# Attention and expert layers in one kernel: all four att-v chunks of a pair in one block, tail scores in a bank of their own

## The chip, the cores and the metric

The kernel runs on one core of a Trainium2 chip. The time is the device time of one execution in microseconds. The engines are named as in the profile: TensorE (PE; PEld is its weight load), VectorE (DVE), ScalarE (ACT), GpSimd (POOL) and SyncE (SP), whose queue issues most transfers. Matrix products write to PSUM, which has eight banks per partition; VectorE and ScalarE read them out.

## The reference, cut to what matters

```python
# q, k, v: 8 batches x 12 heads x 448 positions x 64, fp32
scores = q @ k.T / sqrt(64) - log(448)
attn = 1 / (1 + exp(-scores))                  # a sigmoid, no row sums
x = concat_heads(attn @ v)                     # 3584 tokens x 768
# 8 experts, w1 768 x 1024, w2 1024 x 768
logits = normalise(x) @ normalise(expert_emb).T / tau
e = argmax(logits); gate = softmax(logits)[e]
out = gate * (relu(x @ w1[e]) @ w2[e])         # each token through one expert
```

## The kernel before, in words

**Pairs of heads.** The attention loop runs over 48 pairs: 8 batches times 6 pairs of heads. The 448 positions of a pair are three chunks of 128 and a tail of 64 per head. For a pair i the loop does

- `turn(i + 2, 1)` and `turn(i + 2, 0)` (L336, L327): four fp32 transposes each, for k and for q of the pair after next. VectorE or ScalarE splits the result into a high and a low fp16 part (L344, L346, L347).
- `scores(i, c)` (L358) for c = 0, 1, 2: six products per chunk, three terms for two heads side by side in row halves of the array. ScalarE's sigmoid (L360) reads them out.
- `scores_tail(i)` (L367): three products for the tails of both heads, and their sigmoid (L369).
- `av(i, c)` (L380): fp32 products of the sigmoids with v, two heads side by side in column halves, four chunks (0, 1, 2 and the tail CM = 3) into one accumulator bank.
- `evac(i)` (L394 on ScalarE, L396 on VectorE): the accumulator into xT, high and low part.

Before, chunks 2 and CM of pair i - 1 are multiplied in the loop's pass for pair i, behind its scores 0 and 1; chunks 0 and 1 of pair i come at the end of the pass.

**Work between the pairs.** When the six pairs of a batch are done, `batch_tasks` lists work that the following passes take up, one list each: `chunk` (L402) computes the router's logits of 128 tokens with 12 small products, which VectorE reduces (L404); seven chunks cover two batches. Then `route1` and `route2` (rank products L446, L447), once `select` (L467) and once `early1` (L499) with products that count tokens per expert. `rows` writes token rows to memory with a transposing transfer; `norm` (L421 on VectorE, L424 on ScalarE) squares them. From the fifth batch on, VectorE also casts expert weights: a high part (L170) and a low part (L174), a chunk of 128 rows of w1 or w2 per pass.

**PSUM.** Scores and tail scores take turns in two double banks (`pss`), att-v in two banks (`psv`), and transposes, logits and rank products take turns in two banks that share the tag `tr` (`ptr`, `psl`, `psr`): each new tile takes the bank used longest ago, when its readers are through.

**Order.** In the loop TensorE and SP run in the order in which the program is written. VectorE's, ScalarE's and POOL's queues are ordered by the scheduler. Behind the loop come the first layer-1 halves of two early expert tiles (`layer1_full`, L213; their copies L244 and L246), the last batch's logits and routing, and then 33 expert tiles.

Of the kernel before, what the change touches and what calls it, by code (L numbers as in the profile page):

```python
# [12 lines left out]
F32 = mybir.dt.float32  # L13
I32 = mybir.dt.int32
AF = mybir.ActivationFunctionType
ALU = mybir.AluOpType
AX = mybir.AxisListType
ET = mybir.EngineType
PSUM = bass.MemoryType.PSUM
DRAM = bass.MemoryType.DRAM  # L20

P = 128
CM = 3
# [4 lines left out]
NP = H // 2  # L28
NT = B * S
DM = H * D  # L30
E = 8
# [14 lines left out]
GE = 2  # L46
GC = P * JG
N0 = 4
EG = 5
ORD = "aGbLcdCDAMB"  # L50
ED = 2

# [57 lines left out]
def attn_moe_kernel(ctx: ExitStack, tc: tile.TileContext, q, k, v, emb, tau, w1, w2, consts, eye, out, dbg=None):  # L110
# [3 lines left out]
    dpool = ctx.enter_context(tc.tile_pool(name="dpool", bufs=1, space=DRAM))  # L114
    stg = ctx.enter_context(tc.tile_pool(name="stg", bufs=4))
    ps_s = ctx.enter_context(tc.tile_pool(name="ps_s", bufs=2, space=PSUM))
    ps_v = ctx.enter_context(tc.tile_pool(name="ps_v", bufs=2, space=PSUM))
    mctx = ExitStack()
    ps_m = mctx.enter_context(tc.tile_pool(name="ps_m", bufs=2, space=PSUM))
    wpool = ctx.enter_context(tc.tile_pool(name="wpool", bufs=1))  # L120
# [140 lines left out]
    with ExitStack() as actx:  # L261
# [100 lines left out]

        def scores_tail(i):
            x = kq[i]
            ps = ps_s.tile([P, 2, 512], F32, name="pss")[:, 0, :S]
            for n, (ki, qi) in enumerate(QK_TERMS):
                nc.tensor.matmul(ps, x[:, ki, SM:512], x[:, qi, 512:], start=(n == 0), stop=(n == 2))  # L367
            a = ap2.tile([P, S], F32, name="att_t", bufs=2)
            sig[0] = nc.scalar.activation(a, ps, AF.Sigmoid, bias=bias_s, scale=1.0 / (8.0 * SQK * SQK))  # L369
            aa[i, CM] = a  # L370
# [3 lines left out]
        def av(i, c):  # L374
            if c == 0:
                pav[i] = ps_v.tile([P, 512], F32, name="psv")
            a = aa.pop((i, c))
            for h in range(2):
                w, m = (vv[i][:, h, c, :], a[:, h, :]) if c < CM else (tails[i // TB % 2][2][:, i % TB, h, :], a)
                nc.tensor.matmul(pav[i][h * D:(h + 1) * D, :S], w, m, start=(c == 0), stop=(c == CM))  # L380

        xTs = {}

        def evac(i):
            b, hp = pairs[i]
            ps = pav.pop(i)[:, :S]
            if b % 2 == 0 and hp == 0:
                xTs[b // 2] = ap2.tile([P, JG, 2, NP, P], F16, name="xT")
            x = xTs[b // 2]
            j0 = b % 2 * (CM + 1)  # L390
            parts = ((ps[:, main(b)].rearrange("d (j r) -> d j r", j=CM), [x[:, j0:j0 + CM, ii, hp, :] for ii in range(2)]),
                     (ps[:, tail(b)], [x[:, CM, ii, hp, b % 2 * HP:(b % 2 + 1) * HP] for ii in range(2)]))
            for src, (hi, lo) in parts:
                mark[ET.Activation] = nc.scalar.activation(hi, src, AF.Copy, scale=SX)  # L394
            for src, (hi, lo) in parts:
                mark[ET.DVE] = nc.vector.scalar_tensor_tensor(lo, src, SX, hi, op0=ALU.mult, op1=ALU.subtract)  # L396

        def chunk(g, j):
            ps = ps_m.tile([P, 2 * E], F32, tag="tr", name="psl")
            for kc in range(NKC):  # L400
                for ii in range(2):
                    nc.tensor.matmul(ps, xTs[g][:, j, ii, kc, :], enT[:, kc, :],  # L402
                                     start=(kc == 0 and ii == 0), stop=(kc == NKC - 1 and ii == 1))
            nc.vector.tensor_reduce(L[:, g * JG + j], ps.rearrange("p (i e) -> p e i", i=2), axis=AX.X, op=ALU.add)  # L404
            rowq.append((g, j))

        def rows(g, j):
            xr = xrp.tile([P, 2, DM], F16, name="xrow", bufs=4)
# [123 lines left out]
        def batch_tasks(b):  # L532
            g = b // 2
            if b % 2 == 0:
                return [[lambda j=j: chunk(g, j)] for j in range(3)]
            r = [[lambda: chunk(g, 3), lambda: chunk(g, 4)], [lambda: chunk(g, 5), lambda: chunk(g, 6)],
                 [lambda: route1(g)], [lambda: route2(g)]]
            if g == GS:
                r += [[select]]
            if g == GE:  # L540
                r += [[early1]]
                todo.append((EG, early2))
            return r
# [37 lines left out]
        def task():  # L581
            if later or fill:
                (fill or later).pop(0)()

        with tc.manual_schedule(engines={ET.SP, ET.PE}):
            for i in range(NPAIR):
# [8 lines left out]
                    rows(*rowq.pop(0))  # L595
                scores(i, 0)
                scores(i, 1)
                if i > 0:
                    av(i - 1, 2)
                    av(i - 1, CM)  # L600
                    evac(i - 1)
                if soon:
                    for f in soon.pop(0):
                        f()
                if i + 2 < NPAIR:
                    turn(i + 2, 1)
                task()
                scores_tail(i)
                if i + 2 < NPAIR:
                    turn(i + 2, 0)  # L610
                task()
                scores(i, 2)
                av(i, 0)
                av(i, 1)
                if i + 3 < NPAIR:
                    pack(i + 3, 1)
                    pack(i + 3, 0)
                task()
                if i > 0:
                    b, hp = pairs[i - 1]  # L620
                    if hp == NP - 1:
                        soon = batch_tasks(b)
                if i + 3 == NPAIR:
                    qctx.close()
                    bw = ctx2.enter_context(tc.tile_pool(name="bw", bufs=1, side="right", reuse_waits="tile"))
# [23 lines left out]
        ph[0] = ps_s.tile([P, 2, 512], F32, name="pss")  # L649
        layer1_full(-2, 0, xte[0], 0)  # L650
        hidden(-2, 0)
        for c in (2, CM):
            av(NPAIR - 1, c)
        evac(NPAIR - 1)
        po = {0: [None, None]}
        po[0][0] = ps_v.tile([P, 512], F32, name="psv")
        ph[1] = ps_s.tile([P, 2, 512], F32, name="pss")
# [147 lines left out]

    layer1_full(-1, 0, xte[1], 1)
    hidden(-1, 1)
    po[0][1] = ps_v.tile([P, 512], F32, name="psv")
    hs = [hT.pop((-2, half)) for half in range(2)]
    layer2_full(0, hs, po[0], (0, 3 * NFC // 2))  # L810
    with tc.high_priority():
# [210 lines left out]
```

## Time and profile before

| | us |
|---|---|
| median of 3 runs | 880.82 |
| lowest and highest run | 879.9, 886.85 |
| profiled execution, its own time | 877.93 |
| its span | 876.1 |
| TensorE busy | 826.9 (94%) |
| VectorE busy | 395.7 (45%) |
| ScalarE busy | 398.3 (45%) |

Times in the profile are microseconds from the span's start, unless marked ns. A row of the order of time gives start, length, engine, line and operation, the tiles written and read, shapes, and in brackets the engine's idle time before it with what ended it; neighbouring like instructions are merged (x12). Lengths of TensorE's instructions overlap, since its products are pipelined; the distance between two starts is what a block takes. The attention loop goes from about 10 to 348 us of the span.

### The profile page before, as it was taken

To read this page: it belongs to the slowest core of one execution; us is meant where nothing else is said; L and a number is where in the kernel's file an instruction comes from. 1 tells how busy PE (TensorE), PEld (TensorE's weight loads), DVE (VectorE), ACT (ScalarE), POOL (GpSimd) and SP (SyncE) were. 2 spreads that over 40 slices of the span, in tenths; PEclk is the share of its full clock that TensorE was granted. 3 is DMA by queue.
4 is the path that set the end of the run, shared out by engine and by line. 5 is a ranking of instruction groups with operands and counts; after the bars stand their busy time and mean duration, and the time that the engine had idled before them with its cause. 6 is when DMAs were issued, how large, how long until landed. Compare 5 with 4: busy or idle time off the path is not lost. (4 is left out here: it accounts for less than half of the span.)

```text
span 876.1 us, 16426 instructions
## 1 busy us (share of the span) xinstructions
PE 826.9 (94%) x5384; PEld 402.8 (46%) x5384; DVE 395.7 (45%) x759; ACT 398.3 (45%) x610; POOL 176.7 (20%) x236
## 2 busy tenths in 40 slices
PE   6999999999999999997899999699999999999694
PEld 3444444444444343454455554355555555555352
DVE  4435354446576866775343125643511112525650
ACT  5667677767676766133342123533411112414540
POOL 2112111112121220122212221122222122131101
PEclk9999999999999999999999999799999999999997
DMA  5647485658797986969999589999975569879872
GB/s 149 164 111 198 122 188 156 170 138 204 209 245 196 260 207 174 204 142 240 210 285 172 113 211 245 272 234 275 247 159 122 110 107 250 222 180 263 263 218 42
DMA packets 252599, 168.10 MB, mean 192 GB/s; under 512 B 192412, under 2 KB 229766, under 8 KB 252464
## 3 DMA queue, kind: packets, MB, share of 16 engines
q1 hardware_dynamic: 242272, 131.13, 62.7%
q0 software_dynamic: 9200, 35.03, 13.5%
q8 instruction: 67, 1.10, 0.5%
q14 instruction: 68, 0.56, 0.2%
q10 hardware_dynamic: 992, 0.29, 0.2%
HBM read 103.02 MB, written 23.99 MB: 145 GB/s over the span
## 5 line engine op out<-in xcount | busy, mean ns | idle before, releaser
L213 PE MATMUL pss<-w,xt 128*128 128x512 f16 x900 | 201.3, 383 | 3.6 <-DVE hr L246 3.0
L225 PEld LDWEIGHTS <-hT 128*128 128x128 f16 x1296 | 128.8, 100 | 119.0 <-DMA hT<-hr 22.6
L360 ACT ACTIVATE att<-pss,bias_s 128x896 f32<-128x896 f32 x144 | 139.8, 1004 | 61.5 <-PE pss L358 57.9
L225 PE MATMUL psv<-w,hT 128*128 128x384 f16 x768 | 136.2, 340 | 23.8 <-DMA hT<-hr 19.3
L213 PEld LDWEIGHTS <-xt 128*128 128x128 f16 x900 | 88.1, 99 | 110.6 <-issue 9.7
L380 PE MATMUL psv<-att,vt 128*64 128x448 f32 x576 | 129.4, 556 | 0.0
L244 ACT ACTIVATE hr<-pss 128x512 f16<-128x512 f32 x66 | 36.8, 595 | 191.3 <-PE pss L213 136.3
L246 DVE SCALAR_TENSOR_TENSOR hr<-pss,hr 128x512 f16<-128x512 f32 x66 | 43.3, 687 | 164.7 <-ACT hr L244 150.6
L924 POOL DMA_INDIRECT out<-ob,six x64 | 70.5, 1101 | 204.7 <-ACTq L885 128.5
L358 PE MATMUL pss<-kq 64*128 64x448 f16 x864 | 99.2, 353 | 0.0
L225 PE MATMUL pso<-w,hT 128*128 128x384 f16 x528 | 87.8, 326 | 1.0 <-DMA hT<-hr 1.0
L317 POOL COPY pk<-qk 128x384 f32<-128x384 f32 x94 | 49.2, 525 | 188.2 <-PE ptr L327 111.3
L174 DVE SCALAR_TENSOR_TENSOR w<-stage_w,w 128x768 f16<-128x768 f32 (+1 forms) x78 | 75.7, 1003 | 20.0 <-ACT w L166 16.9
L166 ACT ACTIVATE w<-stage_w 128x768 f16<-128x768 f32 (+1 forms) x78 | 66.4, 878 | 32.1 <-DMA stage_w<-in_moe_w 24.5
L894 POOL DMA_INDIRECT xg<-xs,gix x31 | 32.3, 1041 | 180.5 <-DMA xt<-xg 158.2
L358 PEld LDWEIGHTS <-kq 64*128 64x128 f16 x864 | 34.3, 94 | 63.6 <-issue 41.9
L347 DVE SCALAR_TENSOR_TENSOR kq<-ptr,kq 128x512 f16<-128x512 f32 x96 | 60.1, 647 | 3.3 <-ACT kq L344 3.0
L174 DVE SCALAR_TENSOR_TENSOR w<-stage,w 128x1024 f16<-128x1024 f32 (+1 forms) x48 | 55.1, 1173 | 11.8 <-ACT w L166 10.5
L346 DVE TENSOR_SCALAR kq<-ptr 128x512 f16<-128x512 f32 x48 | 33.0, 687 | 60.7 <-PE ptr L327 60.5
L380 PEld LDWEIGHTS psv<-att,vt 128*64 128x64 f32 x576 | 32.8, 135 | 58.0 <-issue 57.2
L336 PE MATMUL ptr<-ident,pk 128*128 128x128 f32 x288 | 50.5, 286 | 6.1 <-DVE pk L317 4.6
L336 PEld LDWEIGHTS ptr<-ident,pk 128*128 128x128 f32 x288 | 33.6, 144 | 27.5 <-issue 16.4
(189 smaller groups left out, 624.2 us busy)
## 6 DMA issues: line engine op xcount, KB each, us to landing
stage_w<-in_moe_w SPq DMA_DIRECT2D x64, 384.0 KB, 5.3
stage<-in_moe_w SPq DMA_DIRECT2D x40, 512.0 KB, 6.1
qk<-in_q SPq DMA_DIRECT2D x48, 192.0 KB, 3.4
qk<-in_k SPq DMA_DIRECT2D x48, 192.0 KB, 3.4
vt<-in_v SPq DMA_DIRECT2D x48, 192.0 KB, 2.8
xs<-xrow POOLq DMA_DIRECT2D x24, 384.0 KB, 3.6
stage_w<-in_moe_w SPq DMA_DIRECT2D x14, 512.0 KB, 5.1
stage<-in_moe_w SPq DMA_DIRECT2D x8, 384.0 KB, 3.8
```

The costliest lines, as they stand in the source:

```text
L166: nc.scalar.activation(wts[st][i][:, c, :], s, AF.Copy, scale=SW)
L174: nc.vector.scalar_tensor_tensor(wts[st][i + 1][:, c, :], s, SW, wts[st][i][:, c, :], op0=ALU.mult, op1=ALU.subtract)
L213: nc.tensor.matmul(ph[half][:, t % 2], xt[:, xi, kc, :], wts[st][wi][:, kc, half * HF:(half + 1) * HF], start=(n == 0), stop=(n == len(L1_ ...
L225: nc.tensor.matmul(po[d][:, :HD], hs[fc // 4][:, i, fc % 4, :], wts[st][wi][:, fc, d * HD:(d + 1) * HD], start=(n == 0), stop=(n == len(L2 ...
L246: d = nc.vector.scalar_tensor_tensor(hr[:, 1], ps, 0.0, hr[:, 0], op0=ALU.max, op1=ALU.subtract)
L317: en.tensor_copy(t.rearrange("p c h d -> p h c d"), qk[i][:, j])
L336: nc.tensor.transpose(ps[:, o + c * P:o + (c + 1) * P], t[:, c].rearrange("p h d -> p (h d)"), ident)
L347: last_split[0] = nc.vector.scalar_tensor_tensor(lo, ps[:, :n], SQK, hi, op0=ALU.mult, op1=ALU.subtract)
L358: nc.tensor.matmul(ps[:, h, :S], x[r, ki, c * P:(c + 1) * P], x[r, qi, 512:], start=(n == 0), stop=(n == 2))
L360: sig[0] = nc.scalar.activation(a, ps[:, :, :S], AF.Sigmoid, bias=bias_s, scale=1.0 / (8.0 * SQK * SQK))
L380: nc.tensor.matmul(pav[i][h * D:(h + 1) * D, :S], w, m, start=(c == 0), stop=(c == CM))
L924: ins = mark[ET.Pool] = nc.gpsimd.indirect_dma_start(out.rearrange("n (h d) -> (n h) d", h=2), bass.IndirectOffsetOnAxis(ap=six[:, d, c:c ...
```

## The change

Within a pass TensorE's order becomes: scores 0, scores 1, logits or routing work, all eight transposes of the pair after next, tail scores, scores 2, then att-v of the same pair in the order 0, 1, CM, 2, and its copy. The tail scores get a bank of their own (`pst`), for which the att-v accumulator gives up its second one. The two logits chunks that share a pass share one bank and one reduction. An empty list at the head of `batch_tasks`, and EG = 6, keep the router's work in the same passes as before. The last pair's chunks no longer stand between the first two layer-1 halves.

```diff
-EG = 5
+EG = 6
...
-    ps_v = ctx.enter_context(tc.tile_pool(name="ps_v", bufs=2, space=PSUM))
+    ps_v = ctx.enter_context(tc.tile_pool(name="ps_v", bufs=1, space=PSUM))
...
         def scores_tail(i):
             x = kq[i]
-            ps = ps_s.tile([P, 2, 512], F32, name="pss")[:, 0, :S]
+            ps = ps_v.tile([P, 512], F32, name="pst")[:, :S]
...
-                nc.tensor.matmul(pav[i][h * D:(h + 1) * D, :S], w, m, start=(c == 0), stop=(c == CM))
+                nc.tensor.matmul(pav[i][h * D:(h + 1) * D, :S], w, m, start=(c == 0), stop=(c == 2))
...
-        def chunk(g, j):
-            ps = ps_m.tile([P, 2 * E], F32, tag="tr", name="psl")
...
+        def chunk(g, *js):
+            ps = ps_m.tile([P, 2 * E * len(js)], F32, tag="tr", name="psl").rearrange("p (j i e) -> p j i e", i=2, e=E)
...
-                return [[lambda j=j: chunk(g, j)] for j in range(3)]
-            r = [[lambda: chunk(g, 3), lambda: chunk(g, 4)], [lambda: chunk(g, 5), lambda: chunk(g, 6)],
+                return [[]] + [[lambda j=j: chunk(g, j)] for j in range(3)]
+            r = [[], [lambda: chunk(g, 3, 4)], [lambda: chunk(g, 5, 6)],
                  [lambda: route1(g)], [lambda: route2(g)]]
...
                 scores(i, 0)
                 scores(i, 1)
-                if i > 0:
-                    av(i - 1, 2)
-                    av(i - 1, CM)
-                    evac(i - 1)
-                if soon:
+                if soon and i + 1 < NPAIR:
                     for f in soon.pop(0):
                         f()
                 if i + 2 < NPAIR:
                     turn(i + 2, 1)
                 task()
-                scores_tail(i)
                 if i + 2 < NPAIR:
                     turn(i + 2, 0)
                 task()
+                scores_tail(i)
                 scores(i, 2)
-                av(i, 0)
-                av(i, 1)
+                for c in (0, 1, CM, 2):
+                    av(i, c)
+                evac(i)
...
         hidden(-2, 0)
-        for c in (2, CM):
-            av(NPAIR - 1, c)
-        evac(NPAIR - 1)
...
-    po[0][1] = ps_v.tile([P, 512], F32, name="psv")
+    po[0][1] = ps_v.tile([P, 512], F32, name="pst")
```

TensorE's order in a pass without router work, before, from the end of scores 1 on (`pk` holds packed k or q, `tk` and `tq` the tails):

```order
L380 MATMUL psv<-att,vt 64x448 x2
L380 MATMUL psv<-att_t,tv_135 64x448 x2
L336 MATMUL ptr<-ident,pk_651 128x128 x3
L327 MATMUL ptr<-ident,tk_131 128x128
L367 LDWEIGHTS kq
L367 MATMUL pss<-kq 128x448
```

And in the change, from the same place:

```order
L358 LDWEIGHTS kq
L358 MATMUL pss<-kq 128x448
L336 MATMUL ptr<-ident,pk_659 128x128 x3
L327 MATMUL ptr<-ident,tk_131 128x128
L327 MATMUL ptr<-ident,tq_130 128x128
L336 MATMUL ptr<-ident,pk_661 128x128 x3
L367 LDWEIGHTS kq
L367 MATMUL pst<-kq 128x448
```

The two att-v chunks of the older pair are gone from behind the scores, the transposes of q follow those of k, and the tail scores come behind both, in their own bank.

VectorE's queue in the pass with the second logits chunk of the fifth batch (counted from the logits or the copy of att-v that opens it), before:

```order
L404 TENSOR_REDUCE L<-psl 128x8
L396 SCALAR_TENSOR_TENSOR xT<-psv,xT 128x3x128
L396 SCALAR_TENSOR_TENSOR xT<-psv,xT 128x64
L346 TENSOR_SCALAR kq<-ptr 128x512
L170 TENSOR_SCALAR w_0_76<-stage 128x1024
L347 SCALAR_TENSOR_TENSOR kq<-ptr,kq 128x512
L174 SCALAR_TENSOR_TENSOR w_1_77<-stage,w_0_76 128x1024
L347 SCALAR_TENSOR_TENSOR kq<-ptr,kq 128x448
```

And in the change, where the same pass opens with the copy:

```order
L396 SCALAR_TENSOR_TENSOR xT<-psv,xT 128x3x128
L396 SCALAR_TENSOR_TENSOR xT<-psv,xT 128x64
L170 TENSOR_SCALAR w_0_76<-stage 128x1024
L174 SCALAR_TENSOR_TENSOR w_1_77<-stage,w_0_76 128x1024
L405 TENSOR_REDUCE L<-psl 128x8
L346 TENSOR_SCALAR kq<-ptr 128x512
L347 SCALAR_TENSOR_TENSOR kq<-ptr,kq 128x512
L347 SCALAR_TENSOR_TENSOR kq<-ptr,kq 128x448
```

The reduction of the logits (L404, now L405) stood ahead of the copy and of both casts; now it stands behind them. The like holds in nine passes of the change: five with single chunks and two with double chunks of logits, one with rank products (L452) and one with the count of `early1` (L502).

VectorE's queue behind the loop, before (`hr` is the copy of a layer-1 half):

```order
L170 TENSOR_SCALAR w_0_4272<-stage 128x1024 x4
L174 SCALAR_TENSOR_TENSOR w_1_4273<-stage,w_0_4272 128x1024 x4
L246 SCALAR_TENSOR_TENSOR hr_4417<-pss,hr_4417 128x512
L396 SCALAR_TENSOR_TENSOR xT<-psv,xT 128x3x128
L396 SCALAR_TENSOR_TENSOR xT<-psv,xT 128x64
L170 TENSOR_SCALAR w_0_4272<-stage 128x1024
L174 SCALAR_TENSOR_TENSOR w_1_4273<-stage,w_0_4272 128x1024
L246 SCALAR_TENSOR_TENSOR hr_4452<-pss,hr_4452 128x512
L404 TENSOR_REDUCE L<-psl 128x8 x4
```

And in the change:

```order
L396 SCALAR_TENSOR_TENSOR xT<-psv,xT 128x3x128
L396 SCALAR_TENSOR_TENSOR xT<-psv,xT 128x64
L170 TENSOR_SCALAR w_0_4268<-stage 128x1024 x3
L246 SCALAR_TENSOR_TENSOR hr_4413<-pss,hr_4413 128x512
L170 TENSOR_SCALAR w_0_4268<-stage 128x1024
L174 SCALAR_TENSOR_TENSOR w_1_4269<-stage,w_0_4268 128x1024 x4
L246 SCALAR_TENSOR_TENSOR hr_4440<-pss,hr_4440 128x512
L405 TENSOR_REDUCE L<-psl 128x16 x2
```

The four L174 casts stood ahead of the first layer-1 copy; now they stand between it and the second, and the last copy of att-v stands ahead of all.

## Rows read from the trace of the kernel before

**Rows 1.** The page: its span, and busy time, share and instructions of each engine.

```profile
span 876.1 us, 16426 instructions
...
PE 826.9 (94%) x5384; PEld 402.8 (46%) x5384; DVE 395.7 (45%) x759; ACT 398.3 (45%) x610; POOL 176.7 (20%) x236
```

**Rows 2.** Busy time by stretch, one pair: TensorE, loads, VectorE, ScalarE, POOL, clock, DMA.

```profile
200.45:207.26 6.81, 6.81 (x47) 2.86 (x45) 4.39 (x13) 5.29 (x9) 1.58 (x3) 1.00 0.84 218
```

**Rows 3.** TensorE in order of time, the same pair: start, length, instructions.

```profile
200.45 1.31 PE L358 MATMUL pss<-kq 64*128 64x448 f16 x12
201.69 0.97 PE L380 MATMUL psv<-att,vt 128*64 128x448 f32 x4
...
203.34 0.55 PE L336 MATMUL ptr<-ident,pk 128*128 128x128 f32 x3
...
203.84 0.73 PE L367 MATMUL pss<-kq 128*128 128x448 f16 x3
204.40 0.49 PE L336 MATMUL ptr<-ident,pk 128*128 128x128 f32 x3
204.94 0.74 PE L358 MATMUL pss<-kq 64*128 64x448 f16 x6
205.61 1.72 PE L380 MATMUL psv<-att,vt 128*64 128x448 f32 x8
207.26 1.31 PE L358 MATMUL pss<-kq 64*128 64x448 f16 x12
```

**Rows 4.** Order of time in windows under half a us: groups of one att-v block.

```profile
202.49 0.55 PE L380 MATMUL psv<-att_t,tv 128*64 128x448 f32 x2
202.87 0.55 PE L380 MATMUL psv<-att_t,tv 128*64 128x448 f32 x2
```

**Rows 5.** TensorE's waits from 20 to 380 us: total, times, longest.

```profile
PE ptr L327 <- DVE ec L501: 1.2, 1, 1.2
PE psl L402 <- DVE L L404: 0.9, 1, 0.9
PE ptr L336 <- DVE L L404: 0.8, 1, 0.8
```

**Rows 6.** All engines in order of time, where a pair has logits.

```profile
316.97 0.46 PE L402 MATMUL psl<-enT,xT 128*128 128x16 f16 x12
317.11 0.60 ACT L394 ACTIVATE xT<-psv 128x384 f16<-128x384 f32 x2 [0.29 <-PE psv L380]
317.28 0.53 PE L336 MATMUL ptr<-ident,pk 128*128 128x128 f32 x3
...
317.47 0.17 DVE L404 TENSOR_REDUCE L<-psl 128x8 f32<-128x16 f32 x1 [2.62 <-PE psl L402]
```

**Rows 7.** ScalarE and VectorE in order of time, behind att-v of a late pair.

```profile
339.41 0.60 ACT L394 ACTIVATE xT<-psv 128x384 f16<-128x384 f32 x2 [0.28 <-PE psv L380]
...
340.05 0.69 DVE L396 SCALAR_TENSOR_TENSOR xT<-psv,xT 128x384 f16<-128x384 f32 x2 [1.36 <-PE pss L367]
...
340.65 0.68 DVE L170 TENSOR_SCALAR w<-stage 128x1024 f16<-128x1024 f32 x1
...
341.43 1.23 DVE L174 SCALAR_TENSOR_TENSOR w<-stage,w 128x1024 f16<-128x1024 f32 x1
```

**Rows 8.** Groups of VectorE instructions up to 400 us: the casts of w2.

```profile
L174 DVE SCALAR_TENSOR_TENSOR w<-stage,w 128x768 f16<-128x768 f32 x8 | 7.6, 946 | 0.0
...
L170 DVE TENSOR_SCALAR w<-stage 128x768 f16<-128x768 f32 x8 | 5.2, 648 | 0.0
```

**Rows 9.** TensorE in order of time, where a pair has two chunks of logits.

```profile
272.43 0.76 PE L402 MATMUL psl<-enT,xT 128*128 128x16 f16 x24
273.25 0.52 PE L336 MATMUL ptr<-ident,pk 128*128 128x128 f32 x3
```

**Rows 10.** VectorE, then TensorE, in order of time behind the loop.

```profile
348.93 4.62 DVE L174 SCALAR_TENSOR_TENSOR w<-stage,w 128x1024 f16<-128x1024 f32 x4
...
353.81 4.06 PE L213 MATMUL pss<-w,xte 128*128 128x512 f16 x18
```

More of the change, by code (lines that the diff above doesn't have):

```diff
@@ L396, in evac @@
                 mark[ET.DVE] = nc.vector.scalar_tensor_tensor(lo, src, SX, hi, op0=ALU.mult, op1=ALU.subtract)
-        def chunk(g, j):
-            ps = ps_m.tile([P, 2 * E], F32, tag="tr", name="psl")
[L400 to L405, printed above, removed]
+        def chunk(g, *js):
+            ps = ps_m.tile([P, 2 * E * len(js)], F32, tag="tr", name="psl").rearrange("p (j i e) -> p j i e", i=2, e=E)
+            for n, j in enumerate(js):
+                for kc in range(NKC):
+                    for ii in range(2):
+                        nc.tensor.matmul(ps[:, n], xTs[g][:, j, ii, kc, :], enT[:, kc, :],
+                                         start=(kc == 0 and ii == 0), stop=(kc == NKC - 1 and ii == 1))
+            nc.vector.tensor_reduce(L[:, g * JG + js[0]:g * JG + js[0] + len(js)], ps.rearrange("p j i e -> p j e i"), axis=AX.X, op=ALU.add)
+            rowq.extend((g, j) for j in js)
         def rows(g, j):
@@ L618, in attn_moe_kernel @@
                 task()
[L619 to L622, printed above, removed]
+                if pairs[i][1] == NP - 1 and i + 1 < NPAIR:
+                    soon = batch_tasks(pairs[i][0])
                 if i + 3 == NPAIR:
```

## The prediction

> **What bounds the kernel now.** I read the page's head first: TensorE is busy 826.9 of 876.1 us [rows 1], so any change in the attention loop is worth what it does to TensorE's own sequence there. Then the table of busy time by stretch, for one pair in the middle of the loop: 6.81 us long, TensorE busy for all of it at the full granted clock, while VectorE is busy 4.39, ScalarE 5.29 [rows 2]. The reader is to see that in such a pair TensorE waits for nobody. Third, TensorE's order of time for the same pair [rows 3]: scores 0 and 1 from 200.45, four att-v matrices from 201.69, transposes from 203.34, tail scores from 203.84, transposes from 204.40, scores 2 from 204.94, att-v again from 205.61, the next pair at 207.26. So a pair is seven blocks, and their lengths are 1.24, 1.65, 0.50, 0.56, 0.54, 0.67 and 1.65. Last the list of waits: in the whole loop TensorE waits for a reader of a transpose bank only twice, 1.2 and 0.8 us, and once more behind the loop, 0.9 us [rows 5].
>
> The loop therefore gains only where blocks themselves get cheaper, and it loses wherever the new order makes TensorE wait.
>
> **The change part by part.**
>
> *Fewer blocks.* Scores 0 and 1 now go straight into eight transposes, then tail scores, scores 2, and one att-v block of four chunks. No matrix product disappears. Inside an att-v block the instructions come in groups that start 0.38 apart (202.49 to 202.87), but from the last group to the next block it is 0.47 [rows 4], so leaving costs 0.09 to 0.10; a block of two chunks is 1.65 [rows 3] and four groups of 0.375 make 1.50, so entering and leaving cost 0.15 to 0.16 together. Transposes and tail are 1.60 before (0.50 + 0.56 + 0.54); joined they have the same matrices, the same entry and the same step into scores 2, so 1.60 again. The pair goes from two att-v blocks to one: 48 times 0.16 is **-7.7 us**. Lower end: 0.05 each if entering scores from att-v was cheap and transposes from scores are dear, -2.4; upper end 0.20, -9.6. I take 0.16, since it is what the blocks of this very loop show.
> The Trainium skill (TensorEngine Tiling, Key Properties) says that a change of tiling mode drains TensorE. By it only the leaving step would go: the 0.10 of the rows, 48 times, is 4.8 us, and the total below would be 2.9 us higher.
>
> *The banks of the tail scores and of att-v.* The tail scores leave the two score banks, whose waits are nil in the loop, so nothing is gained there. The att-v bank is single now. Its reader must be done before the next pair's att-v begins: ScalarE starts 0.14 after att-v ends (316.97 to 317.11) [rows 6], VectorE 0.64 behind ScalarE (339.41 to 340.05) and is through after 0.60 more (340.65) [rows 7]; that is 1.4 us into the next pair. Att-v now begins after 1.24 + 1.60 + 0.67 = 3.5 us. Price nothing, cover 2.1 us, and VectorE's queue has this read first.
>
> *ScalarE's turn.* Att-v of chunk 2 now needs the sigmoid of the same pair. Its start is 3.5 + 3 x 0.75 + 0.06 = 5.8 us into the pair. ScalarE has, before that sigmoid ends, 5.29 us of work in a pair that also carries a norm [rows 2], beginning at 0.14, and a gap of 0.1 until scores 0 are ready: done at about 5.5. Price nothing; the cover is thin (0.3 us) and is a rival below.
>
> *The transposes' banks.* This is the term that costs. Logits, rank matrices and both transposes share two banks. In a pair with logits the banks go logits, transposes of k, transposes of q; q gets the bank that the logits had, so it waits until VectorE has reduced them. Before, k's transposes and the tail scores stood between (0.50 + 0.56); now only k's transposes. Where VectorE is free this is just enough: the reduction begins 0.50 after the logits do and takes 0.17 [rows 6], over 0.67 after their start; q's turn comes after 0.31 (316.97 to 317.28) [rows 6] plus 0.50.
> But VectorE's order changes too, as the rows of the change show: the weight casts (L170, L174) now stand ahead of the reduction, where before the reduction came first. So in a pair with a cast VectorE is at the att-v copy until 1.4; then L170, 0.78 until the next starts (340.65 to 341.43) [rows 7]; then L174, 1.23 for w1 or 0.95 for w2, where L170 is 0.65 [rows 8]; then the reduction, 0.17. The bank is free at about 3.5 (w1) or 3.1 (w2). Q's transposes would be due at 1.24 + 0.31 + 0.50 = 2.05 with one logits chunk, 2.35 with two, 1.8 with a rank or count matrix. In the new order nine pairs have both: two single chunks beside w1 (1.45 each), one double beside w1 (1.15), one double beside w2 (0.75), two rank or count matrices beside w2 (1.3 each), three single chunks beside w2 (1.05 each): 2.9 + 1.15 + 0.75 + 2.6 + 3.15 = **+10.6 us**. Nothing covers it, since TensorE runs its queue in order: tail scores, scores 2 and att-v stand behind. Lower end 0, if the casts are out of the way; upper end +14, if a cast takes a third of a us longer. I take 10.6, from the durations as they are.
>
> *What goes away.* The two waits of 1.2 and 0.8 [rows 5] belong to pairs counted above: **-2.0**. The double logits had two banks and made k's transposes wait: 0.82 from the 24 small products to them (272.43 to 273.25) [rows 9], against 2 x 0.31 for two singles. With one bank for both, 0.2 goes, six times: **-1.2**.
>
> *The end of the loop.* The 0.9 us wait for the third logits bank [rows 5] goes. Against it, four L174 casts, 4.62 us from 348.93, which ran while the first layer-1 half ran (18 products, 4.06) [rows 10], now stand behind that half's copy and ahead of the reductions, so routing starts over a us later relative to TensorE. TensorE's next layer-1 half, 4.06 again, covers most. Ends -0.9 and +1.6; I take **+0.5**, nearer the casts. The first pair: its tail scores no longer wait for a score bank, but the early transposes wait for the packing instead; nothing, either way within 0.8.
>
> *Queues.* SP issues the same transfers in the same order but for one feed-forward transpose, which now follows four row transposes whose input is ready earlier. Its load of v waits for att-v chunk 2 of an older pair, which now ends about 2 us earlier; so does the row transpose behind it. POOL's row stores stand up to two packs earlier in its queue, and their rows land that much earlier too; POOL is busy 1.58 of 6.81 us [rows 2]. Price nothing. Behind the loop the order of work is the same, so its end moves with the loop's.
>
> **Sum:** -7.7 + 10.6 - 2.0 - 1.2 + 0.5 = +0.2 us on the profiled execution's 877.93. That execution is 2.9 below the median of the runs shown, 880.82; on that scale **881.0 us**, no change. One per cent, 8.8 us, is about what a measurement of this kernel tells from none.
>
> **Rivals.**
> 1. *Faster: the bank of the logits is not late.* If VectorE meets the reduction before the casts bite, or the casts are out before TensorE gets there, only the gains stay: -7.7 - 2.0 - 1.2 + 0.5 = -10.4, **870.4 us**. For it: VectorE has 2.4 us of idle time in the pair shown (6.81 less 4.39). Against it: its order is fixed in its queue, and the time of the casts is in the rows. Chance 0.17, some of it only part of the way.
> 2. *Slower: ScalarE's loop becomes the bound.* With four chunks of one pair in a row, ScalarE goes from the att-v copy through three sigmoids, norm, split and tail sigmoid back to att-v, and att-v back to the copy: 5.29 + 0.14 + 0.1 + 0.85 for the last chunk's products is 6.4 against a pair of 6.65. It decides from 0.25 us of extra hand-offs on. Hand-offs that add 0.65 to the 6.4 would stretch each of the 24 pairs with a norm by 0.4: +9.6, **890.6 us**. For it: no such chain exists in the old order, so no row shows its hand-offs. Against it: ScalarE's idle share and the 0.14 that the rows give for one hand-off. Chance 0.12.
> 3. *The block saves less, or casts hold longer:* the ends of the terms, 886 us, part of the forecast's own range.
>
> **Numbers.** Forecast 0.71, its own range 874 to 888; faster rival 0.17, slower rival 0.12. The 8-in-10 range goes from just above the faster rival's full price to just short of the slower one's: 872 to 889. Faster by over 1% 0.17, within 1% 0.71, slower by over 1% 0.12.
>
> **What would show it.** In the changed profile a plain pair should be 6.65 us long. In nine pairs from the first cast on, the q transposes should show a wait of 0.7 to 1.5 us for VectorE, released by the reduction (L405) or its like, some 10 us in all. Waits of att-v for a sigmoid would speak for rival 2; no waits of the transposes, for rival 1. The prediction is wrong if a plain pair is not shorter, or if the feed-forward part gives back or takes several us through its own stalls.

## The result, and the profile after

The change makes the kernel slower by a little more than one per cent. 890.61 us is the median of 20 runs (884.70 to 896.89, and one of 4598.57), against 880.57 for the kernel before (20 runs, 873.25 to 887.73); the ratio is 1.0118, with a 95% interval of 1.0096 to 1.0140. The ratios, here and below, leave out every run that counts as slow, which is one more than 1.5% above the fastest of its kernel. I had forecast 881.0 and "no change".

The profiled execution of the changed kernel took 895.05 us, 4.4 above its median, and that of the kernel before 877.93, 2.6 below its own. Their spans differ by 17.2 us. Of these, 10.8 are there when the first routed tile begins (its layer 1 starts at 386.59 before and at 397.41 after); the other 6.4 arise in the feed-forward part. That part, from there to the end of the span, took between 480 and 496 us in the traces of this case, with no order by kernel, so the 6.4 are not explained below. The 10.8 are.

The page of the changed kernel first: its span and its engines, as in [rows 1].

```profile
span 893.3 us, 16476 instructions
...
PE 824.8 (92%) x5384; PEld 403.8 (45%) x5384; DVE 402.8 (45%) x751; ACT 397.1 (44%) x610; POOL 183.9 (21%) x236
```

TensorE is busy 2.1 us less, in a span that is 17 us longer: it stands still more. Where the loop has neither logits nor counts it hardly does: after the start the list of its waits has 0.28 us there, in pair 18, for VectorE's copy of att-v. Busy time by stretch of one plain pair (columns as in [rows 2]), and the first and the last rows of TensorE in order of time for the same pair, which answer to [rows 3]:

```profile
197.38:204.05 6.67, 6.67 (x49) 2.89 (x47) 4.24 (x15) 5.19 (x9) 1.70 (x4) 1.00 0.91 233
```

```profile
197.38 1.31 PE L358 MATMUL pss<-kq 64*128 64x448 f16 x12
...
200.89 1.72 PE L380 MATMUL psv<-att,vt 128*64 128x448 f32 x8
202.44 0.92 PE L380 MATMUL psv<-att_t,tv 128*64 128x448 f32 x4
203.19 0.92 PE L380 MATMUL psv<-att,vt 128*64 128x448 f32 x4
204.05 0.74 PE L358 MATMUL pss<-kq 64*128 64x448 f16 x6
```

The pair is 6.67 us long, where 6.81 stood before and 6.65 was forecast. TensorE's waits up to 345 us show where the gain went; [rows 5] is the list that this one answers to. The columns are the wait, the total, the times and the longest.

```profile
PE ptr L327 <- DVE L L405: 5.1, 5, 1.3
...
PE ptr L327 <- DVE ec L502: 3.9, 1, 3.9
PE ptr L336 <- DVE L L405: 1.7, 2, 1.1
PE ptr L327 <- DVE ec L471: 1.3, 1, 1.3
PE ptr L327 <- DVE t L452: 1.1, 1, 1.1
```

These are all transposes that wait for a reader of logits (L405), of a rank matrix (L452), of the early count (L502) or of the selection's count (L471), all on VectorE. The whole list has no wait of TensorE for a sigmoid. Measured from one pair's tail scores to the next, in TensorE's order of time, the pairs are (numbered from 0; the last column is that kernel's own pair of the kind without a wait):

| pairs | before | after | after, no wait |
|---|---|---|---|
| plain | 6.81 | 6.67 | 6.67 |
| 29: selection | 6.83 | 8.62 | 6.68 |
| 32, 33: one logits chunk, w1 cast | 7.11, 7.11 | 8.43, 8.42 | 6.96 |
| 37, 38: two chunks; w1, w2 cast | 7.60, 7.60 | 8.51, 8.11 | 7.34 |
| 40: rank matrix, w2 cast | 6.86 | 8.07 | 6.76 |
| 41: early count, w2 cast | 6.83 | 11.48 | 6.68 |
| 42: early index matrix | 8.83 | 8.43 | 7.28 |
| 43 to 45: one chunk, w2 cast | 7.10, 7.12, 8.08 | 8.03 each | 6.96 |

(Where the changed kernel itself has no such pair without a wait, as for 29, 41 and 42, the value is from the variant with late norms below, or from the one that also has a bank of its own. Before, q's transposes stand behind the tail scores, so the wait of pass 41 for the count, 1.18 us, is in row 42 of that column.)

Up to pair 28 the change is ahead by 4.38 us; at pair 47 it is behind by 7.27 (its tail scores start at 352.44, before at 345.17). The early count, with the pair behind it, costs more than any three others. TensorE and then VectorE in order of time there (times and engines as in [rows 6]):

```profile
302.50 0.18 PE L500 MATMUL psr<-CUM,ones 128*128 128x8 f16 x1
...
307.33 0.48 PE L327 MATMUL ptr<-ident,tq 128*128 128x128 f32 x1 [3.92 <-DVE ec L502]
...
308.24 1.33 PE L367 MATMUL pst<-kq 128*128 128x448 f16 x3
309.50 1.29 PE L358 MATMUL pss<-kq 64*128 64x448 f16 x6
```

```profile
300.59 0.96 DVE L422 TENSOR_TENSOR xf<-xrow 128x768 f32<-128x768 f16 x1 [2.98 <-DMA xrow<-xT]
...
305.06 0.68 DVE L396 SCALAR_TENSOR_TENSOR xT<-psv,xT 128x384 f16<-128x384 f32 x2
305.66 0.55 DVE L170 TENSOR_SCALAR w<-stage 128x768 f16<-128x768 f32 x1
306.24 0.96 DVE L174 SCALAR_TENSOR_TENSOR w<-stage,w 128x768 f16<-128x768 f32 x1
307.12 0.16 DVE L502 TENSOR_TENSOR ec<-psr,eoh 128x8 f32<-128x8 f32 x1
```

VectorE stood idle for 2.98 us in front of the norm's addition (L422), whose transposed row had not landed. Everything behind it was late: the small instructions of the ranks and the early index (L460 and its like, 2.5 us in all), the att-v copy at 305.06, the cast, and only then the count's reader. TensorE's transposes waited 3.92 us. Then it ran at half its clock: by the table of stretches 0.51 (1.2 instead of 2.4 GHz) from 307.30 to 310.70, behind the 1.00 of the stretch up to 306, and the tail scores took 1.33 us instead of 0.73.

```profile
307.30:310.70 3.40, 3.37 (x13) 1.43 (x13) 1.99 (x5) 1.18 (x2) 0.51 (x1) 0.51 0.40 130
```

Last, TensorE behind the loop, which answers to [rows 10]:

```profile
353.79 1.72 PE L380 MATMUL psv<-att,vt 128*64 128x448 f32 x8
355.45 2.98 PE L213 MATMUL pss<-w,xte 128*128 128x512 f16 x13
358.36 0.97 PE L380 MATMUL psv<-att_t,tv 128*64 128x448 f32 x4
359.26 0.39 PE L213 MATMUL pss<-w,xte 128*128 128x512 f16 x1
359.58 0.97 PE L380 MATMUL psv<-att,vt 128*64 128x448 f32 x4
...
371.85 0.20 PE L447 MATMUL psr<-OH,upper 128*128 128x56 f16 x1 [1.36 <-DVE OH L438]
373.03 0.19 PE L448 MATMUL psr<-CUM,ones 128*128 128x56 f16 x1 [0.97 <-DVE CUM L440]
```

The att-v block of the last pair is not one block: 14 products of layer 1 stand between its chunks, so its copy, and with it the routing, comes over 3 us late. From pair 47's tail scores to the first routed tile it is 41.42 us before and 44.97 after.

### The profile page after: what moved, and what is told of

The parts are those of the page before. It is cut to its first block, busy times and chain, and to the rows that moved or that the text cites. A ratio compares the mean times of both kernels' runs of the same rounds, so it can differ in the third digit from the quotient of the medians.

```text
span 893.3 us, 16476 instructions
## 1 busy us (share of the span) xinstructions
PE 824.8 (92%) x5384; PEld 403.8 (45%) x5384; DVE 402.8 (45%) x751; ACT 397.1 (44%) x610; POOL 183.9 (21%) x236
## 5 line engine op out<-in xcount | busy, mean ns | idle before, releaser
L225 PE MATMUL psv<-w,hT 128*128 128x384 f16 x384 | 131.0, 342 | 27.6 <-DMA hT<-hr 17.8
L225 PE MATMUL pst<-w,hT 128*128 128x384 f16 x384 | 130.6, 341 | 0.1
L380 PE MATMUL psv<-att,vt 128*64 128x448 f32 x576 | 127.1, 548 | 0.3 <-DVE xT L396 0.3
L174 DVE SCALAR_TENSOR_TENSOR w<-stage_w,w 128x768 f16<-128x768 f32 (+1 forms) x78 | 76.3, 1004 | 29.0 <-ACT w L166 26.1
L317 POOL COPY pk<-qk 128x384 f32<-128x384 f32 x94 | 54.1, 587 | 164.2 <-issue 72.6
L396 DVE SCALAR_TENSOR_TENSOR xT<-psv,xT 128x384 f16<-128x384 f32 x96 | 33.0, 385 | 87.7 <-PE pss L358 80.9
L394 ACT ACTIVATE xT<-psv 128x384 f16<-128x384 f32 x96 | 29.0, 354 | 94.2 <-PE psv L380 94.2
L380 PEld LDWEIGHTS psv<-att,vt 128*64 128x64 f32 x576 | 36.9, 136 | 63.1 <-issue 46.4
L174 DVE SCALAR_TENSOR_TENSOR w<-stage,w 128x1024 f16<-128x1024 f32 (+1 forms) x48 | 56.3, 1194 | 16.8 <-ACT w L166 15.1
L347 DVE SCALAR_TENSOR_TENSOR kq<-ptr,kq 128x512 f16<-128x512 f32 (+1 forms) x96 | 60.7, 653 | 5.7 <-ACT kq L344 4.6
```

What stands on the lines that cost most here:

```text
L174: nc.vector.scalar_tensor_tensor(wts[st][i + 1][:, c, :], s, SW, wts[st][i][:, c, :], op0=ALU.mult, op1=ALU.subtract)
L225: nc.tensor.matmul(po[d][:, :HD], hs[fc // 4][:, i, fc % 4, :], wts[st][wi][:, fc, d * HD:(d + 1) * HD], start=(n == 0), stop=(n == len(L2 ...
L317: en.tensor_copy(t.rearrange("p c h d -> p h c d"), qk[i][:, j])
L347: last_split[0] = nc.vector.scalar_tensor_tensor(lo, ps[:, :n], SQK, hi, op0=ALU.mult, op1=ALU.subtract)
```

## The experiments

The theories: **A**, TensorE waits because a cast stands ahead of the reader of the bank. **B**, another loop bounds it, and the waits only show where. **D**, the norm's wait for its row holds VectorE's queue. **F**, the layer-1 products between the last att-v chunks make the routing late. Ratios are to the kernel before, in the same runs; a bracket is the 95% interval.

**1. Casts behind.** In the changed kernel:

```diff
-                        fill.append(lambda w=wp.pop(0)[1]: place(w[1:], {**mark, ET.Activation: sig[0]}))
+                        fill.append(lambda w=wp.pop(0)[1]: place(w[1:], {**mark, ET.Activation: sig[0], ET.DVE: last_split[0]}))
```

> The changed kernel with one edit: VectorE's weight casts (L170, L174) are queued behind the last split of k (L347) of the same pair, so the reduction of the logits (L405) and the readers of the rank and count matrices stand ahead of them again. Theory A (the loss is TensorE's wait for a bank whose reader stands behind a cast): of the waits of the transposes in the changed kernel's trace, L405 4.2 + 1.7, L502 3.9 with some 2 us of half clock behind it, L452 1.1, about 11 go; the select pass keeps its 1.6 and the early1 pass some 1.5. That gives 890.6 - 11 = 879.5 us (877 to 882), a plain pair stays 6.67. Rival B (another loop, ScalarE's or the att-v bank's, is the bound, and the waits only show where it bites): 888 to 891, with new waits of TensorE for ScalarE in the same pairs.

Measured 885.11 us, ratio 1.0042 [1.0008, 1.0075]: half of what theory A asked for. The waits for L405 did go (pairs 32, 33, 37, 38, 43 and 44 are 6.96 and 7.34 long), but pair 45 became 10.80. VectorE and TensorE there:

```profile
330.60 0.96 DVE L422 TENSOR_TENSOR xf<-xrow 128x768 f32<-128x768 f16 x1 [5.15 <-DMA xrow<-xT]
331.47 0.62 DVE L347 SCALAR_TENSOR_TENSOR kq<-ptr,kq 128x448 f16<-128x448 f32 x1
```

```profile
332.24 0.88 PE L336 MATMUL ptr<-ident,pk 128*128 128x128 f32 x3 [2.24 <-DVE kq L347]
```

The norm stands ahead of q's split in VectorE's queue and waits 5.15 us for its row; the split frees the bank that the next transposes want. So A holds for the casts. The rest of the loss stands behind norms that wait for rows (the count's pair 41 still takes 9.24 us); that is D, which experiment 5 tests.

**2. Tail scores between the transposes.**

```diff
+                scores_tail(i)
                 if i + 2 < NPAIR:
                     turn(i + 2, 0)
                 task()
-                scores_tail(i)
```

> The changed kernel with the tail scores back between the transposes of k and those of q, nothing else. Theory A: q's turn of the bank comes 0.67 us later in every pair, so each of the ten waits of the transposes shrinks by at most 0.67: 1.3 to 0.65, 0.85 to 0.2, 3.9 to 3.25, together some 6 us: 884.5 us (882 to 887). The plain pair stays 6.67, since transposes and tail scores are the same matrices in the same mode. Rival B: no gain, 889 to 892, and if going in and out of the transposes once more costs 0.1 each, 48 pairs add 5 us: 895.

Measured 885.28 us, 1.0037 [1.0006, 1.0067], the time that theory A asked for. The trace is of its slowest execution, 891.49 us: the waits for the readers of the small results fall from 13.1 to 6.5 us there, as asked, but 3.8 us of waits for VectorE's splits of k and q come in, which theory A didn't have. A plain pair is 6.67 here as well, so the place of the tail scores costs a plain pair nothing. In experiment 3, with the tail scores back in the score banks, it is 6.67 too, and in experiment 4, with the joined order and two att-v blocks, 6.81. So the 0.14 us of a pair belong to the single att-v block.

**3. A bank for the small matrices.** In the loop, logits, rank matrices and counts get the bank that the change gave the tail scores, and these go back to the score banks:

```diff
-            ps = ps_v.tile([P, 512], F32, name="pst")[:, :S]
+            ps = ps_s.tile([P, 2, 512], F32, name="pss")[:, 0, :S]
...
+        def small(n):
+            if inloop:
+                return ps_v.tile([P, 512], F32, name="pst")[:, :n]
+            return ps_m.tile([P, P], F32, tag="tr", name="psr")[:, :n]
...
```

> The changed kernel with the bank of the tail scores given to the logits, the rank matrices and the counts (in the loop), and the tail scores back in the score banks; VectorE's order is unchanged, with the casts ahead of the reductions. Theory A: the transposes have two banks to themselves, so every wait for L405, L452, L471 and L502 goes, 14 us with the half clock: 876.5 us (874 to 880) if the tail scores find their score bank free (sigmoid 0 ends about 1.8 us into the pair, the tail scores start at 2.2, scores 2 at 2.84 against the end of sigmoid 1 at 2.75: up to 0.1 a pair, 5 us, if that is missed). Rival B: 888 to 895, no gain, since the waits move elsewhere.

Measured 877.90 us, 0.9948 [0.9917, 0.9979]: 12.7 below the changed kernel's median, 1.7% by the two ratios. Every wait for L405, L452, L471 and L502 is gone with VectorE's order as it was, so the bank is the link between the casts and TensorE. Some waits behind a late norm stay (VectorE's splits, 2.7 us).

**4. The joined order alone**, in the kernel before (tail scores behind both transposes, nothing else):

> The kernel before with one part of the change alone: the tail scores go behind both transposes instead of between them. VectorE keeps its order there, the reduction ahead of the att-v copy and the casts. Theory A: the joined order alone costs little: the reduction is through 0.67 us after the logits start and q's turn comes after 0.31 + 0.50, so no new wait in plain passes; the two old waits (1.2 and 0.8) may grow by 0.67 each: 880.6 + 1.3 = 882 us (880 to 884). Rival C (the place of the tail scores alone makes q's transposes late, whatever stands in VectorE's queue): nine passes with waits of 0.7 to 1.4, 888 to 891.

Measured 881.17 us, 1.0008 [0.9976, 1.0040]: by time it can't be told from the kernel before. Rival C's nine waits are not there, so C is out. But the joined order isn't free in its trace: two waits, 2.17 us for the count's reader and 2.53 for the logits' in pair 45, make those pairs 9.22 and 9.86 us long, and pair 47 is reached at 350.09, 4.9 us later than before (0.8 of them arise at the start). In both passes VectorE's norm waited for its row ahead of the reader:

```profile
334.20 0.96 DVE L421 TENSOR_TENSOR xf<-xrow 128x768 f32<-128x768 f16 x1 [4.75 <-DMA xrow<-xT]
```

```profile
336.17 0.33 PE L327 MATMUL ptr<-ident,tq 128*128 128x128 f32 x1 [2.53 <-DVE L L404]
```

In the other logits passes the joined order costs nothing. Where a row is late enough, TensorE feels it even though VectorE's reduction still stands ahead of its own pass's cast.

**5. Norms one pair later**, in the changed kernel:

```diff
-            later.append(lambda: norm(g, j, xr))
+            f = lambda: norm(g, j, xr)
+            todo.append((0, lambda: later.append(f))) if inl else later.append(f)
...
-        er, todo = {}, []
+        er, todo, inl = {}, [], [0]
...
+        inl.clear()
```

> The changed kernel with the norm additions (L422) traced one pair later, so that the transposed row they read has a pair more to land; casts and banks as in the change. Theory D (the early count pass cost 3.9 and not 1.3 because VectorE stood 2.98 us in front of a norm whose row had not landed, with the att-v copy, the cast and the count's reader behind it): the count's reader comes some 3 us earlier, the wait of q's transposes there falls from 3.9 to about 1 and the stretch at half clock behind it goes: 890.6 - 5 = 885.6 us (883.5 to 887.5); the waits for L405 stay (some 6 us). Rival E (the eleven small instructions of that pass hold the reader, not the row): 889 to 891.

Measured 882.04 us, 1.0014 [0.9982, 1.0047], more than was asked. VectorE's waits for rows (first fence: changed kernel; second: this one) fall to a third, and the count's wait (third) from 3.92 to 1.46 us, with the full clock behind it:

```profile
DVE xf L422 <- DMA xrow<-xT: 40.9, 22, 3.0
```

```profile
DVE xf L423 <- DMA xrow<-xT: 13.1, 7, 4.0
```

```profile
305.43 0.33 PE L327 MATMUL ptr<-ident,tq 128*128 128x128 f32 x1 [1.46 <-DVE ec L503]
...
305.92 0.73 PE L367 MATMUL pst<-kq 128*128 128x448 f16 x3
```

The selection pair is 6.68 again. Theory D holds for the count and the selection. With the row out of the way the count's reader starts 3.16 us into its pair (305.22, the pair from 302.06), where the prediction had 3.0. In the one trace the gain up to pair 47 is only 3.5 us, since one row landed late even so (a wait of 3.99) and pairs 32 and 33 took 9.80 and 10.02. The rest of the 8.6 between the medians can't be placed by these traces.

**6. Late norms in the kernel before** (the same edit):

> The kernel before with the norm additions one pair later, nothing else. If the wait for the row belongs to the change (there the early count pass met it), the kernel before has little to win: its transposes wait 2.0 us in the loop by its profile, and the att-v copy and the casts stand behind the norm there too: 880.1 - 1.5 = 878.6 us (876.5 to 880.5). If it belongs to both kernels alike, it gains as much as the changed one did, 8.5 us: 871.5.

Measured 878.16 us, 1.0012 [0.9978, 1.0046]: nothing to win. Before, too, VectorE waited for rows (33.4 us in all), but q's transposes came later in the pair and met most readers in time. In this trace pairs 42 and 45 are 0.97 us shorter each than before, and pairs 10 and 22 0.52 longer each. So most of the price of the late rows belongs to the change, and by experiment 4 its joined order is enough to let them through.

**7. Late norms and casts behind**, both, in the changed kernel with its own banks (casts behind k's split only in pairs that have one):

> The changed kernel with late norms, and the weight casts behind k's split in every pair that has one (the last two pairs keep their order). Banks as in the change. Theory A now without the row's wait over it: of the kernel with late norms the waits for L405 (5.8 + 1.7), L453 (1.1) and most of the count's (1.5) go: 882.0 - 9 = 873 us (871 to 876). Rival B (casts in any place hold the queue long enough to cost as much): 878 to 883.

Measured 872.87 us, 0.9879 [0.9828, 0.9931]. That ratio rests on five of the 12 runs, since one of 859.82 us sets its limit low; the medians of all runs, 872.87 and 878.03, give 0.994. With both orders on VectorE mended the change is faster than the kernel before, with no bank moved. At pair 47 it is 6.5 us ahead of the kernel before with late norms (337.95 against 344.48).

**8. The bank and late norms:**

> The kernel with the bank of its own for logits, rank matrices and counts, and the norm additions one pair later as well. Theory D: of that kernel's waits in the loop those for VectorE's splits of k and q (1.8 + 0.9) and its copy of att-v (0.9) follow from waits of the norm for its row, up to 4.4 us long; they go: 877.9 - 3.4 = 874.5 us (872 to 876.5). Rival E: no change, 877 to 879.

Measured 869.84 us, 0.9895 [0.9858, 0.9932], better than was asked. In its loop TensorE waits for VectorE nowhere after the start; the two longest totals of its list of waits up to 345 us are

```profile
PE ptr L336 <- DVE pk L317: 4.7, 1, 4.7
PE pss L367 <- ACT att L360: 1.2, 2, 0.6
```

**9. The last att-v first**, in the changed kernel (last_av is the last product that an att-v block issued):

```diff
...
-        layer1_full(-2, 0, xte[0], 0)
+        with tc.issue_after(last_av[0].ins):
+            layer1_full(-2, 0, xte[0], 0)
```

> The changed kernel with one edit behind the loop: the first half of layer 1 is queued behind the last att-v product, where in the change 13 and 1 of its products stand between the last pair's chunks. Theory F (the 3.5 us that the change loses between the loop's end and the first routed tile come from the last att-v copy, 3.3 us late by those products): the waits behind the loop (1.36, 0.97, 1.43, 1.52) shrink by some 3.5 us together, TensorE waits up to 1 us for the last sigmoids instead: 890.6 - 2.5 = 888 us (886 to 890). Rival G (the casts and the routing chain on VectorE set that stretch): 890 to 892, the same waits.

Measured 886.11 us, 1.0064 [1.0035, 1.0092]. Two of the routing's waits behind the loop (1.36 and 0.97 us) are gone; one of 1.4 us further on, for VectorE's L703, stays. The first of them starts without a wait:

```profile
352.77 7.94 PE L213 MATMUL pss<-w,xte 128*128 128x512 f16 x36
...
365.64 0.19 PE L447 MATMUL psr<-OH,upper 128*128 128x56 f16 x1
```

From pair 47 to the first routed tile it is 42.18 us, 2.8 less than the change's 44.97: theory F. No wait for the last sigmoids took its place. The loop itself is the change's own and reached pair 47 at 348.27, not 352.44. The two executions differ mainly in pairs 18, 29, 41 and 42 (6.67, 7.64, 10.06 and 7.28 here); the norms ahead of the first three waited 0.8 to 2.8 us less for their rows. This execution, 877.54 us, was the fastest of its 12.

**10. All four edits**, and **11. three of them** (bank, late norms, att-v first):

> The changed kernel with four edits: the bank of its own for logits, rank matrices and counts, casts behind k's split, norms one pair later, the first half of layer 1 behind the last att-v. If the waits add up as theories A, D and F have it: 877.9 - 3.4 - 2.5 = 872 us (869 to 875), 1% faster than before. If the feed-forward part gives back what the loop wins (its own stalls for weights and rows do not move with the loop's end), 876 to 880.

> The kernel with a bank of its own for the small matrices and late norms, and the first half of layer 1 behind the last att-v product too. In that kernel's trace the routing behind the loop still shows waits of 1.35 and 0.97 us and 1.5 us more in a stretch at half clock. Theory F: they go, as they did with that edit alone, and 0.5 to 1 comes back as waits for the last sigmoids: 869.8 - 3 = 867 us (865 to 869.5). Rival G (the feed-forward part takes it back): 869 to 872.

Measured 872.48 us, 0.9916 [0.9885, 0.9946], and 870.61, 0.9917 [0.9884, 0.9951]. Neither beats the kernel of experiment 8. All four came out at the forecast number for another reason: without a k split to follow, the last casts piled up ahead of the att-v copy. TensorE waited 2.79 us for its only att-v bank, the granted clock was 0.50 for the 4 us after that, and pair 47 took 12.24 us instead of 6.63. In the kernel of three edits the first routed tile starts 2.3 us earlier than in experiment 8 (378.71 against 381.01), as F asks, and the medians don't show it: the forecast missed there. The feed-forward part differs by more than 2 us between traces, so these runs can't place the difference.

**12. The att-v block in two again**, on the kernel of experiment 8 (q's transposes between chunk 1 and the tail chunk):

> The kernel with the bank of its own and late norms, with q's transposes put between att-v's chunks 0, 1 and the tail chunk, so that att-v is two blocks in a pair again, and no wait of the loop is touched (it has none). It prices the block by itself. By the blocks of the kernel before (0.15 to 0.16 for entering and leaving one): a plain pair goes from 6.67 to 6.82, 46 times, and the time to 869.8 + 6.9 = 876.7 us (875 to 878.5). If only the leaving costs, 0.10: pair 6.77, 874.4. If a block costs nothing and the 0.14 of the pair came from elsewhere: pair 6.67, 869.8.

Measured 898.13 us, 1.0217 [1.0175, 1.0259]; a plain pair took 7.37. The experiment moved more than it was meant to. TensorE in one such pair:

```profile
59.24 0.27 PE L327 MATMUL ptr<-ident,tk 128*128 128x128 f32 x1
59.52 0.73 PE L367 MATMUL pss<-kq 128*128 128x448 f16 x3
60.42 0.74 PE L358 MATMUL pss<-kq 64*128 64x448 f16 x6 [0.17 <-ACT att L360]
61.09 1.72 PE L380 MATMUL psv<-att,vt 128*64 128x448 f32 x8
62.74 0.33 PE L327 MATMUL ptr<-ident,tq 128*128 128x128 f32 x1
...
63.33 0.97 PE L380 MATMUL psv<-att_t,tv 128*64 128x448 f32 x4
64.13 0.92 PE L380 MATMUL psv<-att,vt 128*64 128x448 f32 x4
```

The pieces of att-v give the price that was asked for: the first half takes 1.65 us to the next block instead of the 1.55 in the plain pair above, the tail chunk 0.80 instead of 0.75, so 0.15 for leaving and entering. But tail scores and scores 2 now come half a us earlier, on the score banks: 0.17 of wait at 60.42, and 0.28 from the last k transpose to the tail scores where 0.11 is usual. And the transposes became two blocks too, which I had not counted.

## Why the prediction was wrong, point by point

The ledger, in us on the two profiled executions up to the first routed tile; "measured" is from the table of pairs, each pair less its own kind without a wait:

| term | forecast | measured |
|---|---|---|
| one att-v block instead of two | -7.7 | 46 x -0.145 = -6.7 |
| two logits chunks in one bank | -1.2 | 6 x -0.12 = -0.7 |
| old waits that go (42, 45) | -2.0 | -2.4 |
| eight cast pairs without the count | +9.25 | +9.4 |
| early count | +1.3 | 4.80 + 1.15 = +5.95 |
| selection, and pair 18 | 0 | 1.94 + 0.35 = +2.3 |
| end of the loop | +0.5 | +3.55 |
| sum | +0.2 | +11.4 |

The row of the early count is pairs 41 and 42, and what it holds differs between executions: in experiment 9's trace, whose loop is the same, the count costs 3.38 us and nothing behind it, the selection 0.96 and pair 18 nothing, +4.3 where the ledger has +8.25. The ledger is of an execution 4.4 us above the median.

The trace itself has 10.8 there; the first pair and the last two, which have no transposes, make up the difference.

**The att-v block** was right: forecast 6.65 a pair, 6.67 measured; experiment 2 gives it to the merge alone, and experiment 12 finds 0.10 for leaving and 0.05 for entering. The Trainium skill (TensorEngine Tiling, Key Properties) has the change of tiling mode drain TensorE. I had priced that as the leaving step alone, by which a pair would be 6.71, an estimate; the trace has 6.67. The 0.145 stands nearer to the sum of leaving and entering, as I took it.

**The casts ahead of the reader** were right, by mechanism and by size: 1.47 and 1.46 where I had 1.45, 1.17 for 1.15, 0.77 for 0.75, 1.31 for 1.3, and 1.07 three times for 1.05. Experiments 1, 3 and 7 show the chain from cast to reader to bank to q's transposes: these waits go when the casts go behind the reader, and they go when the bank is no longer shared. Experiment 4 shows that the joined order by itself brings none of them, but for one behind a late row.

**The count pass is the first step that failed.** The words "two rank or count matrices beside w2 (1.3 each)" put both under one price, worked out from busy instructions: att-v copy, cast, reader, the copy done 1.4 us into the pair. The copy began 3.8 us into it (305.06, the pair from 301.26), and TensorE's wait was 3.92. I left out that VectorE can stand idle in its own queue. The list of VectorE's waits of the kernel before has the row that I needed and did not read, and experiments 4 to 6 show that it became dear through the change:

```profile
DVE xf L421 <- DMA xrow<-xT: 33.4, 22, 2.8
```

The same pass of the kernel before, VectorE and then TensorE, shows how far off the price was:

```profile
299.70 0.96 DVE L421 TENSOR_TENSOR xf<-xrow 128x768 f32<-128x768 f16 x1 [0.97 <-DMA xrow<-xT]
...
303.51 0.16 DVE L501 TENSOR_TENSOR ec<-psr,eoh 128x8 f32<-128x8 f32 x1
```

```profile
303.73 0.33 PE L327 MATMUL ptr<-ident,tq 128*128 128x128 f32 x1 [1.18 <-DVE ec L501]
```

The count's reader began 5.09 us into its pair even then (303.51, the pair from 298.42), not 3.0 as in my sum; now it is 5.86 (307.12). Q's turn comes 1.98 us earlier in the pair. The wait grew by these two, 0.77 and 1.98, from 1.18 to 3.92. So the wait of 1.2 that I booked under "what goes away" was the sign of a reader already late, and the change takes away the slack in front of it. The row itself came earlier in the pair than before, as the paragraph on queues had it: the norm began 1.28 us after the pair's start there and 0.67 ahead of it here.

The same oversight made the selection free in my sum: there a norm waits 2.76 us at 210.28, and the copy and the selection's count are late. I also let no wait of TensorE cost more than its own length; behind 3.92 us it ran at half clock, which is the 1.15 of pair 42.

**The end of the loop is the second step that failed:** +0.5 forecast, +3.55 measured. I priced only the casts ahead of the reductions. In the section on the change I wrote that the last pair's chunks no longer stand between the first two layer-1 halves. That holds for the program as written; in TensorE's order 14 layer-1 products now stand between those chunks, which I had not followed. Experiment 9 takes 2.8 us of the 3.55 away.

**The rivals.** The faster one (the bank of the logits not late) fell in the changed kernel but is what experiments 7 and 8 made of it: 872.87 and 869.84, where it said 870.4. The slower one named the measured time (890.6) and was wrong in mechanism; that is chance. ScalarE's loop is no bound: TensorE never waits for a sigmoid in the changed kernel's loop after the start, and the plain pair, norms included, is 6.67. Only experiment 12, where the sigmoids of a pair got less time, has waits of that kind throughout the loop (score banks, 4.9 us in 29 waits).

**Costed at nothing and so found:** the single att-v bank (waits of 0.3 us in all; 2.79 in the kernel of all four edits, behind late casts), ScalarE's turn, and the first pair (0.2 us the other way).

What stays open: how the 10.0 us between the medians divide among these terms, since the ledger is of one pair of executions; why late norms alone gain 8.6 us between medians when their trace shows 3.5 up to the loop's end, and what makes the feed-forward part differ by up to 16 us between traces.

## What to carry to other kernels

When a change puts a consumer closer to its producer in one engine's order, read the other engine's queue for everything that now stands ahead of the reader: its busy instructions, and the ones that wait there for a DMA. The second kind is in that engine's own list of waits, not in the list of the engine that bounds. And a small result that shares a ring of buffers with a large stream lends its lateness to the stream: a bank of its own was worth 12.7 us here between medians, and together with the norms' later place the change wins 1% instead of losing 1.2%.

## What the runs showed of the hardware

A wait of TensorE can cost more than itself. Behind 3.92 us of waiting the granted clock was 0.51 for 3.4 us, and behind a wait of 2.00 us in the kernel of experiment 5 it was 0.60 from 236.00 to 238.00 (first fence). The length of the wait alone doesn't decide it: behind 3.17 us in the kernel of experiment 9 the clock stayed at 1.00 for the next 4 us (second fence). In the kernel of experiment 1 it stayed at 1.00 behind 2.34 us and was 0.50 for 4 us behind 2.24.

```profile
236.00:238.00 2.00, 2.00 (x13) 0.70 (x11) 1.57 (x3) 1.18 (x2) 0.51 (x1) 0.60 1.13 197
```

```profile
304.73:308.73 4.00, 4.00 (x25) 1.81 (x27) 1.89 (x5) 2.18 (x3) 0.51 (x1) 1.00 0.53 172
```

Where TensorE's loop no longer waits for VectorE, it repeated almost exactly in two executions: the kernels of experiments 8 and 11, which share their loop, reach pair 47 at 336.18 and 336.17 us. The loop of the changed kernel reached it at 352.44 in its own execution and at 348.27 in that of experiment 9, which shares it.
